# Two chains per pair of heads on TensorE, key tiles of 112, and fewer transfers in an attention and feed-forward kernel

## The chip, the cores and the metric

The kernel runs on one core of a Trainium2 chip. Its engines are TensorE (PE in the rows, PEld for its weight loads), VectorE (DVE), ScalarE (ACT), GpSimd (POOL) and SyncE (SP), which here issues every DMA. The metric is the device time of one execution in microseconds; less is better. PE's clock has two levels, 1.2 and 2.4 GHz, and the profile gives the granted level of a stretch as a share of the higher one.

## The reference

For 8 batches of 12 heads, 448 rows of 64 elements, everything in float32:

```
q_n, k_n = rmsnorm(q, g_q), rmsnorm(k, g_k)
scores = q_n @ k_n.T / sqrt(64);  scores -= max(scores, axis=-1)
attn = exp(scores);  attn /= sum(attn, axis=-1) + 1e-9
x = attn @ v                       # heads side by side: 3584 tokens of 768
h = x @ w_in                       # 768 -> 2048
out = (h * cos(h)) @ w_out         # 2048 -> 768
```

## The kernel before

Heads are taken two at a time: 48 pairs, six to a batch. A pair has its two heads on the two halves of the 128 partitions (64 each), and two matmuls of 64 rows, one per half, run beside each other on PE.

For a pair u the program does, on PE:

- **rough scores** R (`rough`, tile SA): q_hi times k_hi, one tile of queries after the other. VectorE takes each row's maximum (`rowmax`, tile sm), turns it (`m_turn`), and it goes through DRAM (`m_store`, `m_load`) into a row, tile mr.
- **scores** S (`score`, tile ST): keys on the partitions, queries along the row. Four matmuls add up: k_hi q_hi, k_hi q_lo, k_lo q_hi, and minus the maximum from mr. ScalarE writes the exponential (`expo`, tiles P0 to P3).
- **P v** (`av`, tile O): float32, so each matmul goes through the array more than once. The 64 columns of each head stand beside each other.
- **sums** (`total`, tile T): ones times P. From the seventh pair on VectorE first adds the four P tiles (`p_sum`). The sum goes through DRAM twice for its reciprocal (`t_store`, `t_load`, `i_store`, `rs_load`).

The key axis of 448 is cut into three tiles of 128 and a rest of 64. The rest of both heads shares a fourth tile, as a 128-row matmul of 448 columns; for it, q and k lie in DRAM and in SBUF with 576 columns, the rest repeated. S and T share two PSUM tiles of two banks each, R has one such tile of its own, and O and the feed-forward tile ph have one bank each.

Between these, PE runs the first feed-forward matrix (`ffn1`, tile ph, called F below): 128 rows by 128 columns, three matmuls for each product of split operands. A batch has 16 blocks of 18 matmuls, 48 to a pair. F of a batch runs while the next batch's pairs are attended; that of the last batch follows alone. Then a second phase (tiles y, lines from 587 on) applies the cosine and the second matrix.

No loop sets the order of the first phase. Every step is given to a planner (class `Plan`) with an engine, a cost and a due time; the planner goes through time by its costs, and on each engine takes, among the steps whose inputs are ready, the one that is due first. The result is one fixed order for each engine and for SP's queue, each of which runs strictly in it. Four numbers at the head of the plan set the due times: BASE, PER0, PER1 and PER, the start of a pair's scores.

Of the kernel before, what the change touches and what calls it, by code (L numbers as in the profile page):

```python
# [27 lines left out]
class Plan:  # L28
# [5 lines left out]

    SIGNAL = 0.16
    LEAD = 0.3

    def __init__(self, rings, apart=False):
        self.rings = rings
        self.parts = []  # L40
        self.start = []
        self.lead = []
        self.writer = {}
        self.readers = {}
        self.users = {}
        self.apart = apart
        self.issue = set()

    def add(self, eng, cost, due, fn, *args, r=(), w=(), land=0.0, start=0.0, lead=None):
        n = len(self.parts)  # L50
        deps = set()
# [19 lines left out]
        self.lead.append(self.LEAD * (eng == PE) if lead is None else lead)  # L71

    def order(self):
# [23 lines left out]
        self.busy = dict.fromkeys(free, 0.0)  # L97
        while True:
# [16 lines left out]
            n = heapq.heappop(can[e])[1]  # L115
            cost, fn, args, land = (parts[n][i] for i in (1, 3, 4, 6))
            end = free[e] = t + cost
# [16 lines left out]
def tile_attention_moe(  # L134
# [3 lines left out]
    qT: bass.AP,  # L138
    kT: bass.AP,
# [10 lines left out]
    W = kT.shape[2]  # L150
    NT = S // 128
    REST = S - 128 * NT
    NC = 2 * NT + 1

    NFIRST = 2
    NSUM = NP
# [26 lines left out]
    m_d = dpool.tile([NU, REST + 2 * S], F32, tag="m_d", name="m_d")  # L183
# [15 lines left out]
    less, less_r = (apool.tile([128, 128], F32R, tag=n, name=n, bufs=1) for n in ("less", "less_r"))  # L199
    for t in (less, less_r):  # L200
        nc.gpsimd.memset(t.bitcast(F32), 0.0)
        for hh in range(2):
            cs = slice(0, 128) if t is less else slice(64 * hh, 64 * hh + 64)
            nc.gpsimd.memset(t.bitcast(F32)[64 * hh : 64 * hh + 1, cs], -1.0)
    sms = [apool.tile([128, 32], F32, tag=f"sm{i}", name=f"sm{i}", bufs=1) for i in range(2)]
    mrs = [apool.tile([128, S], F32R, tag=f"mr{i}", name=f"mr{i}", bufs=1) for i in range(2)]
# [6 lines left out]
    def g_fold():  # L213
# [119 lines left out]
    def first_load(u):  # L333
        t = tl(u, "sd", [128, 14, D], F32, "P2")
# [27 lines left out]
    def first_copy(u, c, hh):  # L362
        name = "qk"[c] + "d"
        if hh == 0:
            x = tl(u, name, [128, W], F32)
            nc.gpsimd.memset(x[:, S:W], 0.0)
        x = pair[u][name][64 * hh : 64 * hh + 64]
        src = pair[u]["turn", c][:D, S * hh : S * hh + S]
        rest = slice(S + REST * hh, S + REST * hh + REST)
        if hh == 0:  # L370
            nc.vector.tensor_copy(x[:, :S], src)
            nc.vector.tensor_copy(x[:, rest], src[:, S - REST :])
        else:
            nc.scalar.copy(x[:, :S], src)
            nc.scalar.copy(x[:, rest], src[:, S - REST :])
# [7 lines left out]
    def r_load(u, c):  # L383
        dst = tl(u, ("rqb", "rkb")[c], [128, W], F32)
        for hh in range(2):
            p, n = slice(64 * hh, 64 * hh + 64), S * hh + S
            nc.sync.dma_start(dst[p, :S], row(r_d[u, c], n - S, n).broadcast_to([64, S]))
            rest = row(r_d[u, c], n - REST, n).unsqueeze(1).broadcast_to([64, 2, REST])
            nc.sync.dma_start(dst[p, S:].rearrange("p (a n) -> p a n", a=2), rest)  # L389

    def k_load(u):
        nc.sync.dma_start(tl(u, "kd", [128, W], F32), kT[u])

    def k_norm(u):
        kd = pair[u]["kd"]
        nc.gpsimd.tensor_tensor(kd, kd, pair[u].pop("rkb"), ALU.mult)  # L396

    def k_high(u):
        nc.scalar.copy(tl(u, "khi", [128, W], F32R), pair[u]["kd"])  # L399

    def k_low(u):
        d = pair[u]
        nc.gpsimd.tensor_tensor(tl(u, "kl", [128, W], F32R), d.pop("kd"), d["khi"].bitcast(F32), ALU.subtract)  # L403

    def q_load(u):
        nc.sync.dma_start(tl(u, "qd", [128, W], F32), qT[u])

    def q_norm(u):
        qd = pair[u]["qd"]
        nc.gpsimd.tensor_tensor(qd, qd, pair[u].pop("rqb"), ALU.mult)  # L410

    def q_high(u):
        nc.scalar.activation(tl(u, "qhi", [128, W], F32R), pair[u]["qd"], AF.Copy, scale=gsc)

    def q_low(u):
        d = pair[u]
        nc.vector.scalar_tensor_tensor(
            tl(u, "ql", [128, S], F32R), d.pop("qd")[:, :S], gsc, d["qhi"].bitcast(F32)[:, :S], op0=ALU.mult, op1=ALU.subtract
        )

    def v_load(u):
        nc.sync.dma_start(tl(u, "vs", [128, 2 * NT + 1, D], F32), v[u])


    def own(t, hh):
        return t[64 * hh : 64 * hh + 64, :S]

    def tiles(t, j, hh):
        return t[:, S:] if j == NT else t[64 * hh : 64 * hh + 64, 128 * j : 128 * j + 128]

    def rough(u, j):
        d = pair[u]
        t = d["SA", j] = double(ps_a, "SA", f"SA{u}_{j}")
        if j == NT:
            nc.tensor.matmul(t[:, 0, :S], tiles(d["qhi"], j, 0), d["khi"][:, :S], start=True, stop=True)
            return
        for hh in range(2):
            nc.tensor.matmul(t[:, hh, :S], tiles(d["qhi"], j, hh), own(d["khi"], hh), start=True, stop=True)  # L438

    def rowmax(u, j):  # L440
        t, sm = pair[u].pop(("SA", j)), sms[u % 2]
        if j < NT:
            nc.vector.tensor_reduce(sm[:, j : NC : NT + 1], t[:, :, :S], axis=AX.X, op=ALU.max)  # L443
        else:
            nc.vector.tensor_reduce(sm[:, j : j + 1], t[:, 0, :S], axis=AX.X, op=ALU.max)
# [4 lines left out]
    def m_store(u):  # L450
        mt = pair[u].pop("mt")
        m = m_d[u][: 2 * S].rearrange("(c p) -> c p", p=128)
        for p in range(0, 128, 32):
            nc.sync.dma_start(m[:, p : p + 32], mt[p : p + NC])
        for p in range(64, 128, 32):
            nc.sync.dma_start(row(m_d[u], 2 * S + p - 64, 2 * S + p - 32), mt[p + NT : p + NT + 1])

    def m_load(u):
        for hh in range(2):
            n = (S + REST) * hh  # L460
            nc.sync.dma_start(mrs[u % 2].bitcast(F32)[64 * hh : 64 * hh + 1], row(m_d[u], n, n + S))

    def score(u, j):
        d, mr = pair[u], mrs[u % 2]
        t = d["ST", j] = double(ps_s, "ST", f"ST{u}_{j}")
        for n, (a, c) in enumerate((("khi", "qhi"), ("khi", "ql"), ("kl", "qhi"), (None, None))):
            for hh in range(1 if j == NT else 2):
                if j == NT:
                    out, st, mv = t[:, 0, :S], tiles(d[a], j, 0) if a else less_r, d[c][:, :S] if c else mr
# [582 lines left out]
```

## Time and profile before

| | us |
|---|---|
| median of 3 runs | 1544.09 (1537.98 to 1549.36) |
| the profiled execution | 1546.6 |
| its span, first to last instruction | 1544.8 |
| granted clock of PE over the span | 0.968 |
| first matmul of F | 137.14 |
| first matmul of the second phase | 1128.15 |

The span has a first phase of 1128 us and a second of 417 us. Of the first, the 137 us before F begins hold the first six pairs. A row of the timeline gives the start, the length as modelled (matmuls overlap, so the step from one start to the next is what one costs), the engine, the line, and in brackets how long the engine was idle before and what ended that.

### The profile page before, as it was taken

The page shows a single profiled execution, that of the slowest core. Times are in us where ns is not written, and L with a number is a line of the kernel's source. Part 1 is how long each engine was busy: PE and PEld are TensorE (multiplying, and loading weights), DVE is VectorE, ACT ScalarE, POOL GpSimd, SP SyncE. Part 2 cuts the span into 40 slices and gives each one's busy share as a digit, 9 for nine tenths or more (in the row PEclk, how much of TensorE's full clock was granted, in tenths as well). Part 3 has the DMA queues.
Part 4 walks back from the last instruction along what each step waited for, and adds up shares of the span by engine and source line. Part 5 has one row for each costly group of instructions (what it writes and reads, how often), then busy time and mean ns, then how long its engine had stood idle before and what let it go on. Part 6 is the DMA issues. An engine that isn't in the chain of part 4 may idle for free.

```text
span 1544.8 us, 21497 instructions
## 1 busy us (share of the span) xinstructions
PE 1452.5 (94%) x7060; PEld 1041.2 (67%) x7060; DVE 973.0 (63%) x1255; ACT 781.3 (51%) x1212; POOL 905.0 (59%) x600
## 2 busy tenths in 40 slices
PE   3987889999999999999999999999999999999999
PEld 2433455656656666665666666567988999999998
DVE  7536769555666676556674757521787877868911
ACT  3543434444444444444444434323867777778732
POOL 6756657664585767576746454501138576585674
PEclk6998789999999999999999999999999999999999
DMA  5555663445646566566664555314957958859463
GB/s 164 136 151 180 195 215 113 126 136 156 188 128 223 176 195 186 179 198 192 186 186 135 186 174 165 116 55 150 346 180 256 323 167 292 290 171 336 165 209 107
DMA packets 187264, 287.09 MB, mean 186 GB/s; under 512 B 69968, under 2 KB 133648, under 8 KB 187152
## 3 DMA queue, kind: packets, MB, share of 16 engines
q1 hardware_dynamic: 187152, 285.72, 58.5%
q8 instruction: 55, 0.90, 0.3%
q14 instruction: 57, 0.47, 0.1%
HBM read 222.38 MB, written 63.25 MB: 185 GB/s over the span
## 4 chain that ended last, share of the span: by engine, by line
PE 65%; DMA 12%; DVE 8%; SPq 5%; POOL 4%; issue 4%; ACT 2%; DVEq 0%; POOLq 0%; ACTq 0%
PE ph L572 9%; PE ST L473 8%; PE y L651 8%; PE y L652 8%; PE y L650 8%; PE ph L574 7%; PE ph L573 7%; PE O L500 6%; DMA ti<-t_d 2%; DMA rawo<-w_out 2%; PE SA L438 2%; PE T L514 2%; DVE P L489 2%; DVE sm L443 2%; SPq L389 1%
## 5 line engine op out<-in xcount | busy, mean ns | idle before, releaser
L572 PE MATMUL ph<-xs,wi 128*128 128x448 f32 x768 | 309.3, 403 | 4.7 <-ACT he L584 3.9
L573 PE MATMUL ph<-xs,wi 128*128 128x448 f32 x768 | 283.4, 369 | 1.8 <-POOL xs L558 1.8
L574 PE MATMUL ph<-xs,wi 128*128 128x448 f32 x768 | 283.8, 369 | 0.0
L651 PE MATMUL y<-glo,wo 128*128 128x448 f32 x672 | 246.2, 366 | 1.3 <-POOL glo L635 1.3
L650 PE MATMUL y<-ghi,wo 128*128 128x448 f32 x672 | 245.8, 366 | 0.0
L652 PE MATMUL y<-ghi,wo 128*128 128x448 f32 x672 | 245.8, 366 | 0.0
L443 DVE TENSOR_REDUCE sm<-SA 128x2 f32<-128x896 f32 x144 | 156.3, 1086 | 123.4 <-PE SA L438 122.7
L572 PEld LDWEIGHTS ph<-xs,wi 128*128 128x128 f32 x768 | 145.1, 189 | 123.2 <-issue 78.7
L480 ACT ACTIVATE P<-ST 128x896 f32<-128x896 f32 x144 | 131.6, 916 | 136.5 <-PE ST L473 136.4
L500 PE MATMUL O<-P,vs 128*64 128x448 f32 (+1 forms) x768 | 185.9, 569 | 0.0
L485 DVE TENSOR_TENSOR P<-P,P 128x896 f32<-128x896 f32 x84 | 106.5, 1268 | 125.0 <-PE O L500 86.1
L584 ACT COPY he<-ph 128x448 f32<-128x448 f32 x128 | 68.1, 532 | 185.7 <-PE ph L574 143.1
L574 PEld LDWEIGHTS ph<-xs,wi 128*128 128x128 f32 x768 | 146.0, 190 | 13.3
L573 PEld LDWEIGHTS ph<-xs,wi 128*128 128x128 f32 x768 | 146.2, 190 | 10.7 <-POOL xs L558 2.1
L651 PEld LDWEIGHTS y<-glo,wo 128*128 128x128 f32 x672 | 126.2, 188 | 13.5 <-POOL glo L635 2.9
L652 PEld LDWEIGHTS y<-ghi,wo 128*128 128x128 f32 x672 | 126.2, 188 | 10.5
L650 PEld LDWEIGHTS y<-ghi,wo 128*128 128x128 f32 x672 | 126.2, 188 | 10.5
L330 POOL TENSOR_TENSOR r<-r,nhalf 128x14 f32<-128x14 f32 (+1 forms) x50 | 129.8, 2597 | 5.6 <-DVE r L350 2.1
L403 POOL TENSOR_TENSOR kl<-kd,khi 128x576 fp32r<-128x576 f32 x48 | 72.6, 1514 | 96.5 <-ACT khi L399 85.0
L410 POOL TENSOR_TENSOR qd<-qd,rqb 128x576 f32<-128x576 f32 x46 | 72.3, 1572 | 73.4 <-DMA i_d<-ti 20.1
L547 POOL TENSOR_TENSOR xf<-xf,rs 128x448 f32<-128x448 f32 x48 | 59.7, 1244 | 78.8 <-DMA rs<-i_d 62.8
L396 POOL TENSOR_TENSOR kd<-kd,rkb 128x576 f32<-128x576 f32 x46 | 71.7, 1558 | 52.4 <-DMA kd<-kT 21.3
(234 smaller groups left out, 2641.6 us busy)
## 6 DMA issues: line engine op xcount, KB each, us to landing
wo<-wo_d SPq DMA_DIRECT2D x88, 768.0 KB
h_d<-he SPq DMA_DIRECT2D x128, 224.0 KB
hb<-h_d SPq DMA_DIRECT2D x128, 224.0 KB
wo_d<-wv SPq DMA_DIRECT2D x56, 384.0 KB
sd<-sd SPq DMA_DIRECT2D x46, 448.0 KB
kd<-kT SPq DMA_DIRECT2D x46, 288.0 KB
qd<-qT SPq DMA_DIRECT2D x46, 288.0 KB
raw<-w_in SPq DMA_DIRECT2D x16, 768.0 KB
```

Source lines behind the costliest of these rows:

```text
L330: nc.gpsimd.tensor_tensor(r, r, nhalf.broadcast_to([128, c1 - c0]), ALU.pow)
L443: nc.vector.tensor_reduce(sm[:, j : NC : NT + 1], t[:, :, :S], axis=AX.X, op=ALU.max)
L473: nc.tensor.matmul(out, st, mv, start=(n == 0), stop=(n == 3))
L480: nc.scalar.activation(tl(u, f"P{j}", [128, 2, S], F32), t[:, :, :S], AF.Exp)
L485: nc.vector.tensor_tensor(d["P0"], d["P0"], d[f"P{step}"], ALU.add)
L500: nc.tensor.matmul(d["O"][64 * hh : 64 * hh + 64, :S], st, mv, start=(j == 0), stop=(j == NT))
L572: nc.tensor.matmul(ph[:, :S], whi, x2[:, 0, :], start=(cc == 0), stop=False)
L573: nc.tensor.matmul(ph[:, :S], whi, x2[:, 1, :], start=False, stop=False)
L574: nc.tensor.matmul(ph[:, :S], wlo, x2[:, 0, :], start=False, stop=(cc == NCC - 1))
L650: nc.tensor.matmul(y, whi, hi, start=(k == 0 and chain < 2), stop=False, skip_group_check=chain == 2)
L651: nc.tensor.matmul(y, whi, lo, start=False, stop=False, skip_group_check=chain == 2)
L652: nc.tensor.matmul(y, wlo, hi, start=False, stop=(k == NH - 1), skip_group_check=chain == 2)
```

## The change

Six things are changed, all in the first phase:

- **Planner.** A step on PE can now name the step that should follow it at once (`after`); PE waits up to PATIENCE for that one. Steps have a mode, F, H (64-row matmuls) or C (P v and sums), and a change of mode costs SWITCH in the plan. P v of a pair is one step (`av_all`). From the seventh pair on, sums, P v and the first three rough tiles of the pair after next follow each other; so do the fourth rough tile of the next pair and the four score tiles of this one.
- **Tiles.** The key axis is cut into four tiles of 112; all score and rough matmuls are now pairs of 64 rows by 112 columns. The repeated rest is gone, q and k have 448 columns, and P tiles have 112 partitions.
- **PSUM.** Rough scores, scores and sums share three tiles of two banks; O and ph share two single banks.
- **Sums.** VectorE's sums go to a tile of their own, PS, and no longer into P0.
- **Transfers.** q and k come in one DMA, their norms in two, not eight; the maxima are stored in one, not six, and the sums in one, not two. Over the program SP issues 1163 DMAs where it issued 1773.
- **Plan.** Due times, costs, the ring sizes and the places at which a pair's preparation is due are other numbers; there are eight xf tiles, not six.

The diff, cut to its core:

```diff
+    PATIENCE = 0.6
+    SWITCH = {("F", "H"): 0.2, ("H", "F"): 0.2, ("F", "C"): 0.15, ("C", "F"): 0.2, ("H", "C"): 0.15, ("C", "H"): 0.2}
...
-                if can[e]:
+                if e == PE and hold is not None:
+                    limit = free[e] + self.PATIENCE
+                    t = max(free[e], ready[hold]) if not left[hold] and ready[hold] <= limit else limit
+                elif can[e]:
...
-    NT = S // 128
-    REST = S - 128 * NT
-    NC = 2 * NT + 1
+    NT = 4
+    T = S // NT
+    NC = 2 * NT
...
-    ps_a = att.enter_context(tc.tile_pool(name="ps_a", bufs=1, space=PSUM))
-    ps_s = att.enter_context(tc.tile_pool(name="ps_s", bufs=2, space=PSUM))
-    ps_o = att.enter_context(tc.tile_pool(name="ps_o", bufs=1, space=PSUM))
-    ps_h = att.enter_context(tc.tile_pool(name="ps_h", bufs=1, space=PSUM))
+    ps_s = att.enter_context(tc.tile_pool(name="ps_s", bufs=3, space=PSUM))
+    ps_o = att.enter_context(tc.tile_pool(name="ps_o", bufs=2, space=PSUM))
...
     def m_store(u):
-        mt = pair[u].pop("mt")
-        m = m_d[u][: 2 * S].rearrange("(c p) -> c p", p=128)
-        for p in range(0, 128, 32):
-            nc.sync.dma_start(m[:, p : p + 32], mt[p : p + NC])
-        for p in range(64, 128, 32):
-            nc.sync.dma_start(row(m_d[u], 2 * S + p - 64, 2 * S + p - 32), mt[p + NT : p + NT + 1])
+        nc.sync.dma_start(m_d[u].rearrange("a c i -> (a c) i"), pair[u].pop("mt"))
...
-            for hh in range(1 if j == NT else 2):
-                if j == NT:
-                    out, st, mv = t[:, 0, :S], tiles(d[a], j, 0) if a else less_r, d[c][:, :S] if c else mr
-                else:
-                    out, st = t[:, hh, :S], tiles(d[a], j, hh) if a else less[64 * hh : 64 * hh + 64]
-                    mv = own(d[c] if c else mr, hh)
-                nc.tensor.matmul(out, st, mv, start=(n == 0), stop=(n == 3))
+            for hh in range(2):
+                st = own(d[a], hh, j) if a else own(less, hh)
+                nc.tensor.matmul(t[:T, hh, :S], st, own(d[c], hh) if c else mr[64 * hh : 64 * hh + 64, :, :T], start=(n == 0), stop=(n == 3))
...
+    def av_all(u):
+        for j in range(NT):
+            av(u, j)
...
-    BASE, PER0, PER1, PER = 30.0, 18.0, 19.0, 19.0
-    SPLIT = 54.0
+    BASE, PER0, PER1, PER = 30.0, 14.0, 18.5, 18.7
+    SPLIT = 50.0
+    AFTER = 9.0
...
     for u in range(NU):
-        spots += [("S", u, 0), ("S", u, 1)] + [("T", u - 1, 0)] * (u > NSUM) + [("S", u, 2), ("S", u, 3)]
+        spots += [("S", u, j) for j in range(NT)] + [("T", u, 0)] * (u >= NSUM)
+        spots += [("R", u + 2, j) for j in range(NT)] * (u + 2 < NU)
...
+            last = add(PE, 0.82, D0 + 0.8 * j, score, u, j, r=[(n, u) for n in ("khi", "kl", "qhi", "ql", "mr")], w=key,
+                       mode="H", after=last if j else link.pop("R", None))
...
+            n = add(PE, 0.75, D1, total, u, 0, 1, r=[("PS", u)], w=key, mode="C")
+            r = [k for p in P for k in p]
+            link["C"] = add(PE, 2.97, D1, av_all, u, r=r + [("vs", u)], w=[singles["O", u]], mode="C", after=n)
```

How this moves PE's instructions, in the middle of the first phase. A name ends in the pair's and the tile's number: SA34_2 is the rough tile 2 of pair 34, ST33_0 the score tile 0 of pair 33, T32 and O33 sums and P v, ph4_3 block 3 of F in batch 4. PE before, around the scores of pair 33; left out at each mark are matmuls of F, or the other three matmuls of a score tile:

```order
L438 MATMUL SA34_2_6614<-khi34_6340,qhi34_6444 128x448 x2
L473 MATMUL ST33_0_6619<-qhi33_6239,khi33_6134 128x448 x2
...
L572 MATMUL ph4_3_6631<-xs_677,wi3_1144 128x448
...
L435 MATMUL SA34_3_6644<-khi34_6340,qhi34_6444 128x448
...
L473 MATMUL ST33_1_6661<-qhi33_6239,khi33_6134 128x448 x2
...
L514 MATMUL T32_6679<-P032_6462,ones_100 64x448 x2
L500 MATMUL O33_6686<-P033_6638,vs33_6396 64x448 x2
...
L473 MATMUL ST33_2_6711<-qhi33_6239,khi33_6134 128x448 x2
...
L500 MATMUL O33_6686<-P133_6682,vs33_6396 64x448 x2
```

The same engine now, from the sums of pair 33 to the scores of pair 34:

```order
L490 MATMUL T33_6455<-PS33_6387,ones_94 64x448 x2
L479 MATMUL O33_6461<-P033_6358,vs33_6102 64x448 x2
...
L438 MATMUL SA35_0_6474<-khi35_6199,qhi35_6210 112x448 x2
...
L438 MATMUL SA35_2_6488<-khi35_6199,qhi35_6210 112x448 x2
L552 MATMUL ph4_5_6492<-xs_622,wi5_1023 128x448
...
L438 MATMUL SA35_3_6529<-khi35_6199,qhi35_6210 112x448 x2
L462 MATMUL ST34_0_6533<-qhi34_6034,khi34_6026 112x448 x2
...
L462 MATMUL ST34_1_6543<-qhi34_6034,khi34_6026 112x448 x2
```

What was spread among pieces of 6 or 12 matmuls of F is now two runs, with 18 to 36 matmuls of F between them. Counted through the whole order, PE goes 708 times from one of the shapes F, 64-row or P v to another before, and 239 times after; of these, 185 and 49 lead into P v or sums.

SP's queue in the startup, before, from one pair's maxima (mt3, stored through m_d) to the next store:

```order
L387 DMA rkb5_614<-r_d_86 64x448
L389 DMA rkb5_614<-r_d_86 64x2x64
...
L454 DMA m_d_87<-mt3_612 7x32 x4
L456 DMA m_d_87<-mt3_612 1x32 x2
L525 DMA ti1_661<-t_d_88 112x8
L387 DMA rqb5_668<-r_d_86 64x448
...
L378 DMA r_d_86<-r6_580 128x2x7
L315 DMA sd8_686<-sd 128x896
```

The same place now:

```order
L402 DMA rb5_552<-r_d_80 64x2x448 x2
L448 DMA m_d_81<-mt3_565 128x32
L335 DMA sd7_593<-sd 128x896
L504 DMA ti1_596<-t_d_82 112x8
L393 DMA r_d_80<-r6_567 128x2x7
L454 DMA mr1_103<-m_d_81 1x16x32 x2
```

One store and one pair of loads of norms stand where six and eight issues stood.

## Rows read from the trace of the kernel before

**Rows 1.** Windows: length; busy PE, PEld, DVE, ACT, POOL; PE clock, DMA share, GB/s.

```profile
0.00:137.00 137.00, 97.30 (x460) 46.37 (x461) 75.27 (x103) 60.27 (x89) 89.00 (x81) 0.84 0.55 161
137.00:300.00 163.00, 142.48 (x647) 85.51 (x647) 123.83 (x132) 73.54 (x105) 105.80 (x72) 0.89 0.52 163
300.00:1040.00 740.00, 715.73 (x3536) 456.99 (x3534) 448.34 (x527) 319.50 (x516) 425.69 (x313) 0.99 0.54 166
...
1128.00:1545.00 417.00, 411.68 (x2018) 378.09 (x2016) 281.89 (x423) 279.67 (x422) 273.51 (x129) 1.00 0.68 224
```

**Rows 2.** Timeline of ACT: the copied sums of pairs 12 and 46.

```profile
298.23 0.54 ACT L517 ACTIVATE ts<-T 128x448 f32<-128x448 f32 x1
...
1032.16 0.54 ACT L517 ACTIVATE ts<-T 128x448 f32<-128x448 f32 x1
```

**Rows 3.** Timeline of PE in the middle of the first phase.

```profile
600.00 0.36 PE L574 MATMUL ph<-xs,wi 128*128 128x448 f32 x1
600.29 0.47 PE L473 MATMUL ST<-qhi,khi 64*128 64x448 f32 x2
600.60 0.36 PE L473 MATMUL ST<-ql,khi 64*128 64x448 f32 x2
...
601.00 0.37 PE L473 MATMUL ST<-mr,less 64*128 64x448 f32 x2
601.29 0.97 PE L514 MATMUL T<-P,ones 128*64 128x448 f32 x4
602.10 0.92 PE L500 MATMUL O<-P,vs 128*64 128x448 f32 x4
602.95 0.47 PE L572 MATMUL ph<-xs,wi 128*128 128x448 f32 x1
603.26 0.37 PE L573 MATMUL ph<-xs,wi 128*128 128x448 f32 x1
```

**Rows 4.** Lines of PE, 300 to 1040 us: busy, mean; idle before them.

```profile
L438 PE MATMUL SA<-khi,qhi 64*128 64x448 f32 x198 | 46.0, 460 | 4.1 <-DVE sm L443 3.5 <-ACT qhi L413 0.6
L435 PE MATMUL SA<-khi,qhi 128*128 128x448 f32 x33 | 14.8, 449 | 17.7 <-DVE sm L443 17.6
```

**Rows 5.** Timeline of PE in the startup.

```profile
36.45 0.91 PE L473 MATMUL ST<-mr,less 64*128 64x448 f32 x2 [3.75 <-DMA mr<-m_d]
...
61.77 0.47 PE L438 MATMUL SA<-khi,qhi 64*128 64x448 f32 x2
63.44 0.47 PE L435 MATMUL SA<-khi,qhi 128*128 128x448 f32 x1 [1.19 <-DVE sm L443]
...
66.11 0.92 PE L473 MATMUL ST<-mr,less 64*128 64x448 f32 x2 [1.39 <-DMA mr<-m_d]
66.65 0.75 PE L473 MATMUL ST<-qhi,khi 64*128 64x448 f32 x2
...
134.25 0.93 PE L473 MATMUL ST<-mr,less 64*128 64x448 f32 x2 [4.21 <-DMA mr<-m_d]
```

**Rows 6.** Timeline of SP's queue in the startup.

```profile
72.02 1.60 SPq L454 DMA_DIRECT2D m_d<-mt  x4
...
78.40 0.58 SPq L461 DMA_DIRECT2D mr<-m_d  x2
```

**Rows 7.** Lines by shape, the whole span: busy, mean ns; idle before them.

```profile
L443 DVE TENSOR_REDUCE sm<-SA 128x2 f32<-128x896 f32 x144 | 156.3, 1086 | 123.4 <-PE SA L438 122.7
L485 DVE TENSOR_TENSOR P<-P,P 128x896 f32<-128x896 f32 x84 | 106.5, 1268 | 125.0 <-PE O L500 86.1 <-ACT P L480 38.5
L489 DVE TENSOR_TENSOR P<-P,P 64x448 f32<-64x448 f32 x84 | 93.5, 1113 | 7.4 <-ACT P L478 5.1
L445 DVE TENSOR_REDUCE sm<-SA 128x1 f32<-128x448 f32 x48 | 29.8, 621 | 38.7 <-PE SA L435 38.6
...
L480 ACT ACTIVATE P<-ST 128x896 f32<-128x896 f32 x144 | 131.6, 916 | 136.5 <-PE ST L473 136.4
L478 ACT ACTIVATE P<-ST 128x448 f32<-128x448 f32 x48 | 26.1, 543 | 70.4 <-PE ST L473 70.2
```

More of the change, by code (lines that the diff above doesn't have):

```diff
@@ L47, in __init__, with add @@
         self.issue = set()
-    def add(self, eng, cost, due, fn, *args, r=(), w=(), land=0.0, start=0.0, lead=None):
+        self.mode = {}
+        self.follow = {}
+    def add(self, eng, cost, due, fn, *args, r=(), w=(), land=0.0, start=0.0, lead=None, mode=None, after=None):
         n = len(self.parts)
+        self.mode[n] = mode
+        if after is not None:
+            self.follow[after] = n
         deps = set()
@@ L97, in order @@
         self.busy = dict.fromkeys(free, 0.0)
+        mode, hold, done = None, None, set()
         while True:
@@ L114, in order @@
                 heapq.heappush(can[e], (parts[n][2], n))
-            n = heapq.heappop(can[e])[1]
-            cost, fn, args, land = (parts[n][i] for i in (1, 3, 4, 6))
+            if e == PE and hold is not None:
+                n, hold = hold, None
+                if left[n] or ready[n] > t:
+                    continue
+                can[e].remove((parts[n][2], n))
+                heapq.heapify(can[e])
+            else:
+                n = heapq.heappop(can[e])[1]
+            cost, fn, args, land = (parts[n][i] for i in (1, 3, 4, 6))
+            if e == PE and self.mode[n]:
+                cost += self.SWITCH.get((mode, self.mode[n]), 0.0)
+                mode = self.mode[n]
+            if e == PE:
+                done.add(n)
+                hold = self.follow.get(n)
+                hold = None if hold in done else hold
             end = free[e] = t + cost
@@ new lines, in prepare @@
+        sd, r, rb, qk = ([(n, u)] for n in ("sd", "r", "rb", "qk"))
+        add(SP, ISS, D0 - 42, st_load, u, w=sd, land=6.5)
+        add(SP, ISS, D0 - 26, qk_load, u, w=[("qk", u, 0), ("qk", u, 1)], land=LAND)
+        add(ACT, 0.95, D0 - 34, st_square, u, w=sd)
+        add(DVE, 1.08, D0 - 33, st_reduce, u, r=sd, w=r)
+        add(POOL, 0.35, D0 - 32, st_mean, u, w=r)
+        add(POOL, 2.7, D0 - 31, st_pow, u, 0, 14, w=r)
+        add(SP, ISS, D0 - 27, st_store, u, r=r, w=[("rd", u)], land=LAND)
@@ L825, in attend @@
-        add(SP, 2 * ISS, D1 + 12, rs_load, u, r=[("id", u)], w=[("rs", u)], land=5.0)
+        P = [[(f"P{j}", u + NFIRST * (j == 0))] for j in range(NT)]
+        for j in range(NT):
+            key = [spots["S", u, j]]
+            last = add(PE, 0.82, D0 + 0.8 * j, score, u, j, r=[(n, u) for n in ("khi", "kl", "qhi", "ql", "mr")], w=key,
+                       mode="H", after=last if j else link.pop("R", None))
+            add(ACT, 0.92, D0 + 0.8 * j + 1, expo, u, j, r=key, w=P[j])
+            if j and u >= NSUM:
+                add(DVE, 1.25, D0 + 0.8 * j + 3, p_sum, u, j, r=P[j] + P[0] * (j == 1), w=[("PS", u)])
@@ L840, in multiply @@
                 r += [("xs", cc, s) for cc in (2 * part, 2 * part + 1) for s in range(2)]
[L841 removed]
+                add(PE, 1.225, d, ffn1, b, fc, part, ps_o, "S1", r=r, w=[key], mode="F")
             add(ACT, 0.53, d - 4, h_out, b, fc, r=[key], w=[("he", NFC * b + fc)])
             add(SP, ISS, d, h_store, b, fc, r=[("he", NFC * b + fc)], land=LAND)
[L845 to L846 removed]
+    for u in range(NFIRST):
+        first(u)
     for fc in range(NFC):
```

300 lines of the change are left out of this document (122 added, 178 removed), and 6 rows, old and new, of the table RING.

## The prediction

> **What bounds the kernel now.** I read the windows by stage first, then the lines of each engine, then PE's own timeline, because only a timeline shows what PE does between matmuls that all count as busy.
>
> The windows [rows 1] show three stages. Up to 137 us PE is busy 97.30 us at a granted clock of 0.84: the startup is bound by latency. From 300 to 1040 us it is busy 715.73 of 740 us (97%) at 0.99, so there PE is the bound, and DVE (448.34, 61%), POOL (58%) and ACT (43%) are not. From 1128 us on is the second phase, 417 us, of which the change touches nothing. The rate of the middle stage is read from ACT: the copied sums of pairs 12 and 46 stand at 298.23 and 1032.16 us [rows 2], 733.93 us for 34 pairs, 21.59 us each.
>
> But busy is not at its peak. In PE's timeline [rows 3] matmuls of one shape start 0.20 us apart: two concurrent 64-row matmuls of a score tile (600.60, then two steps to 601.00) just as one 128-row matmul of F. Where the shape changes, the step is longer. From F to scores it is 0.29 us (600.00 to 600.29), and the first step inside the scores 0.31 (to 600.60): 0.09 to leave and 0.11 to enter, 0.20 in all. From P v to F the same: the first step of F is 0.31 (602.95 to 603.26). Into sums or P v it is 0.09 and 0.05: sums take 0.81 us after a change (601.29 to 602.10), where P v that follows without one takes 0.85 with its own 0.09 to leave in it, so 0.76. A change costs 0.14 us if it leads into P v or sums, and 0.20 otherwise.
>
> **The change, part by part.**
>
> *Changes of shape (term 1).* PE's order has 708 of them before, 185 into P v or sums: 185 × 0.14 + 523 × 0.20 = 130.5 us. After it has 239, 49 of them into P v or sums: 6.9 + 38.0 = 44.9 us. Since PE is the bound, nearly all of that is on the path. Term 1 is **-86 us**. At 0.15 for each of the 469 it would be -70, at 0.20 throughout -94.
>
> *Matmuls themselves.* A pair had three 64-row tiles and one 128-row tile, and now has four 64-row tiles. Both kinds step by 0.20, so rough scores keep 4 steps and scores 16. P v and sums keep their number too. Nothing.
>
> *Startup (term 2).* PE waits there for the maxima's way through DRAM five times, from 3.75 us at 36.45 to 4.21 at 134.25 us, 14.7 us together [rows 5]; it waits 1.19 us for each row maximum, since R has one tile; and after a wait the clock is low (matmuls last 0.75 us at 66.65, not 0.36). SP is the cause of much of it: the store of the maxima is six issues, four of which take 1.60 us, and their load is issued 6.4 us after the store began (72.02 to 78.40) [rows 6]. The change issues 610 fewer DMAs, at the 0.40 us of one of those four. It has the rough scores of a pair ready one pair earlier, and three tiles, so that rough tiles no longer wait for each other. Against it: F now begins after eight pairs, not six, so PE has nothing to fill with for longer; two pairs more at the old share of idle (39.7 us in the first 137) would cost some 10 us. Between all of the waits gone with their clock, -30, and +10, I take **-13 us**, about the five waits.
>
> *Waits of R and S (term 3).* From 300 to 1040 us PE's idle is 24.3 us, and 21.8 of it is R waiting, nearly all for the row maximum [rows 4]. With three tiles that goes: **-22 us**. In its place comes a new wait. The three tiles are now also those of S: the third score tile takes the place of the fourth rough tile, which runs just ahead of the first, so its row maximum must be done by then. From one R to the next through the maximum is 1.67 us with DVE free (61.77 to 63.44) [rows 5]; PE gives it 0.20 for R and two score tiles of four steps of 0.20, 1.80 in all: 0.13 us to spare. DVE is busy 61% of the time with instructions of 0.85 us (448.34 over 527 [rows 1]), so the maximum finds half of one ahead of it in most pairs, sometimes two: 0.4 us for each of the 42 pairs from the seventh on, **+17 us**. Bounds: nothing, and a whole sum of 1.27 us [rows 7] less the 0.13, 48 us. Behind S wait only F and the next chain on PE. ACT's exponentials start late with it, and DVE's sums and T after them, but 36 matmuls of F, 7.3 us, lie between S and T, against an exponential of 0.92 and a sum of 1.27 after the last score.
>
> *Other engines.* A row maximum of the fourth tile goes from 0.62 to 1.09 us and its exponential from 0.54 to 0.92. The sums on VectorE go from 2 × 1.27 + 2 × 1.11 to 3 × 1.27, so DVE has 0.5 us less for a pair and ACT 0.4 more [rows 7]. They have 39% and 57% of the stage free: nothing. If the pair falls to 19.5 us, DVE stands at 65%. POOL's three operations on 576 columns now have 448, less too.
>
> A rule speaks against the new tiles. Trainium Kernel Development and Optimization of the Trainium skill, Best Practices, says always to tile to 128 partitions; by it 16 of 128 lanes lie idle in every tile of 112, and the 0.84 us more of maximum and exponential would be the price, 40 us over 48 pairs if they were on the path. The rows have it the other way: the old cut spent its fourth tile on 448 columns in three engines, and what it saved there was hidden under PE.
>
> *Sum.* -86 - 13 - 22 + 17 = -104. The profiled execution took 1546.6 us, so 1442.6; the median of the runs lies 2.5 us below it: **1440 us**. As a check, by the pair: ten changes of shape less at 0.185 on average is 1.85 us, the R waits 0.64, the new one 0.4: 21.59 becomes 19.5.
>
> **The rivals.**
>
> *Round trips take what PE gives back (chance 0.12).* A pair's norms, maxima and sums go through DRAM four times, in order, in one queue. At a shorter pair one of them comes too late: the reciprocal of the pair before stands on DVE between the sums of this one and waits for its load, then T waits. For it speaks that the startup shows PE waiting on such a trip at 16 us a pair (36.45 to 134.25 us are six pairs) [rows 5]. Against it: from 300 us on, PE's idle has 2.5 us left for everything but R's waits, and SP has 13 issues less for a pair. If 1.4 us for each of 42 pairs goes back to waiting, 59 of the 104 us are lost: 1499. The Trainium skill (DMA: Bandwidth & Descriptors, Rules for kernel authors) says that a transfer whose outermost dimension is under 16 is confined to that many DMA engines; the new load of the maxima is cut 4 by 4 by 32, the store of the sums into two rows, so by that rule both could land later than the old ones. No row of this case shows it.
>
> *The third score tile stalls PE (0.04).* The mechanism of term 3 at full size: row maxima queue behind decodes and sums on DVE, S stalls in every pair, and the clock falls after it, as at 66.65 us [rows 5]. It decides from 2.9 us a pair on, where 42 pairs eat the 121 us that terms 1 to 3 give without it. At 3.5 us of wait and 1 of slow clock, less the 0.4 counted, it is +172: 1612 us, slower. Against it: DVE has 39% free, and its maxima of a pair stand nearly side by side in its order.
>
> *The changes of shape cost nothing (0.06).* If the longer steps were only how starts are recorded, term 1 is nothing and -18 is left: 1526 us, 1.2% faster, on the edge. Against it: 0.20 us between starts is the rate of a long run of F, and after a change no later start catches up [rows 3]. By TensorEngine Tiling of the Trainium skill, Key Properties, switching the tiling mode drains the engine and going to another tile of a mode does not; by that rule, the trace agrees.
>
> **How the numbers follow.** The forecast has 0.78. Its own range, from -94 - 30 - 22 at one end to -70 + 10 - 22 + 48 at the other, is 1398 to 1510, most of it under 1485. For 8 in 10 I give 1400 to 1515, which takes in most of the forecast and the first rival. About 1%, 15 us, is what a measurement here can tell from no change. Faster by more: the forecast, the first rival and half of the third, 0.91 with some room; slower by more 0.04; within 1% 0.05.
>
> **What would show it.** Term 1: in the steady stretch PE's long steps at only five places of a pair, and copied sums about 19.5 us apart. Term 2: F beginning about when it does now, with eight pairs done and not six. Term 3: PE's idle under the score line, released by the row maximum, of 10 to 25 us in all, and none left under the rough line. The second phase should take its 417 us, beginning near 1025. It is wrong if the pairs stay above 20.5 us apart: then idle under T (late sums, the reciprocal ahead of them) is the first rival, idle over 2 us under S the second, and no idle with short steps the third.

## The result, and the profile after

The changed kernel takes 1415.69 us (median of 4 runs, 1412.94 to 1416.9) against 1545.53 on the same chip: 0.9163 of the time (95% interval 0.9124 to 0.9202). The forecast was 1440, the range 1400 to 1515. The profiled execution took 1412.94 us, its span is 1411.2.

The windows after, cut where F begins (138), at the copied sum of pair 12 (243), at the end of the steady pairs and where the second phase begins (996), columns as in [rows 1]:

```profile
0.00:138.00 138.00, 106.29 (x592) 58.05 (x592) 105.89 (x130) 76.46 (x108) 105.70 (x88) 0.91 0.68 203
138.00:243.00 105.00, 93.75 (x502) 65.06 (x502) 91.79 (x90) 53.67 (x78) 84.76 (x57) 0.93 0.52 155
243.00:905.00 662.00, 653.82 (x3744) 467.03 (x3740) 424.04 (x497) 321.03 (x519) 403.40 (x314) 1.00 0.58 174
...
996.00:1412.00 416.00, 410.29 (x2020) 378.38 (x2018) 281.49 (x422) 279.19 (x422) 273.30 (x129) 1.00 0.67 225
```

In the steady stretch PE now lacks 8.2 us of 662, not 24.3 of 740. The startup has a higher clock (0.91 and 0.93, before 0.84 and 0.89) and is shorter. The second phase is what it was. The copied sums of pairs 12 and 46 in ACT's timeline, which answer to [rows 2]:

```profile
242.59 0.54 ACT L497 ACTIVATE ts<-T 128x448 f32<-128x448 f32 x1 [0.34 <-PE T L490]
...
896.98 0.55 ACT L497 ACTIVATE ts<-T 128x448 f32<-128x448 f32 x1 [2.82 <-PE T L490]
```

They are 654.4 us apart: 19.25 us a pair, before 21.59. PE's timeline, which answers to [rows 3], through the rough tiles of a pair and into its chain of scores:

```profile
600.66 0.37 PE L554 MATMUL ph<-xs,wi 128*128 128x448 f32 x1
600.95 0.87 PE L438 MATMUL SA<-khi,qhi 64*112 64x448 f32 x6
601.75 0.47 PE L552 MATMUL ph<-xs,wi 128*128 128x448 f32 x1
602.06 0.36 PE L553 MATMUL ph<-xs,wi 128*128 128x448 f32 x1
...
604.38 0.46 PE L438 MATMUL SA<-khi,qhi 64*112 64x448 f32 x2
604.67 0.37 PE L462 MATMUL ST<-qhi,khi 64*112 64x448 f32 x2
604.87 0.36 PE L462 MATMUL ST<-ql,khi 64*112 64x448 f32 x2
605.07 0.37 PE L462 MATMUL ST<-qhi,kl 64*112 64x448 f32 x2
605.27 0.37 PE L462 MATMUL ST<-mr,less 64*112 64x448 f32 x2
```

Three rough tiles stand together and pay one way in and one out: 0.29 us from F (0.20 without a change), 0.80 for the three (0.60), 0.31 for F's first step, 0.40 in all. The groups of PE's lines, first from 243 to 905 us, which answer to [rows 4]:

```profile
L462 PE MATMUL ST<-qhi,khi 64*112 64x448 f32 x280 | 55.9, 395 | 6.4 <-DVE sm L442 3.2 <-ACT P L466 3.2
...
L438 PE MATMUL SA<-khi,qhi 64*112 64x448 f32 x272 | 45.3, 409 | 0.5 <-DVE sm L442 0.4
L490 PE MATMUL T<-PS,ones 112*64 112x448 f32 x136 | 33.0, 563 | 0.6 <-DVE PS L472 0.6
```

and then the startup, 0 to 243 us, which answers to [rows 5]:

```profile
L462 PE MATMUL ST<-mr,less 64*112 64x448 f32 x104 | 24.0, 445 | 1.9 <-DMA mr<-m_d 1.9
...
L438 PE MATMUL SA<-khi,qhi 64*112 64x448 f32 x112 | 22.0, 467 | 23.8 <-DVE sm L442 15.0 <-ACT ts L497 4.7 <-ACT qhi L419 4.0
```

R no longer waits in the steady stretch, and the idle time of the new wait, under the scores, is 6.4 us. Up to pair 12 PE waits once for the maxima's way through DRAM, 1.9 us. Before, it waited for it seven times up to there, 18.3 us: the five times of [rows 5], 14.7 us, and two more after 137 us.

By stage, the prediction's terms (0.185 us a change on average; 98 fewer changes up to pair 12, 352 in the 34 pairs to pair 46, 19 after) against the two profiled executions:

| | forecast | measured |
|---|---|---|
| up to pair 12 | -18 - 13 = -31 | 298.2 to 242.6: -55.6 |
| pairs 12 to 46 | -65 - 22 + 14 = -73 | 733.9 to 654.4: -79.5 |
| pair 46 to the second phase | -3 + 3 = 0 | 96.0 to 99.5: +3.5 |

Most of what the forecast missed lies in the startup. Whether the terms were right one by one, or only in their sum, is for experiments to tell.

### The profile page after: what moved, and what is told of

It reads as the page before. It is cut to its first block, busy times and chain, and to the rows that moved or that the text cites. A ratio compares the mean times of both kernels' runs of the same rounds, so it can differ in the third digit from the quotient of the medians.

```text
span 1411.2 us, 21112 instructions
## 1 busy us (share of the span) xinstructions
PE 1355.1 (96%) x7300; PEld 1050.3 (74%) x7300; DVE 948.4 (67%) x1209; ACT 780.9 (55%) x1208; POOL 878.1 (62%) x593
## 4 chain that ended last, share of the span: by engine, by line
PE 73%; DVE 8%; DMA 7%; POOL 6%; issue 3%; ACT 2%; SPq 1%; ACTq 0%; DVEq 0%; POOLq 0%
PE ST L462 9%; PE ph L552 9%; PE y L631 9%; PE y L632 9%; PE y L630 9%; PE ph L554 8%; PE ph L553 8%; PE O L479 8%; PE T L490 3%; PE SA L438 2%; DMA h_d<-he 2%; DVE sm L442 2%; DMA ti<-t_d 2%; POOL qk L409 1%; POOL r L350 1%
## 5 line engine op out<-in xcount | busy, mean ns | idle before, releaser
L442 DVE TENSOR_REDUCE sm<-SA 112x2 f32<-112x896 f32 x192 | 198.5, 1085 | 156.8 <-PE SA L438 156.5
L552 PE MATMUL ph<-xs,wi 128*128 128x448 f32 x768 | 291.2, 379 | 0.0
L554 PE MATMUL ph<-xs,wi 128*128 128x448 f32 x768 | 281.4, 366 | 0.0
L553 PE MATMUL ph<-xs,wi 128*128 128x448 f32 x768 | 281.3, 366 | 0.0
L466 ACT ACTIVATE P<-ST 112x896 f32<-112x896 f32 x192 | 166.7, 920 | 64.1 <-PE ST L462 62.0
L479 PE MATMUL O<-P,vs 112*64 112x448 f32 x768 | 156.2, 541 | 0.6 <-ACT he L564 0.6
L350 POOL TENSOR_TENSOR r<-r,nhalf 128x14 f32<-128x14 f32 (+1 forms) x50 | 135.6, 2714 | 6.4 <-DVE r L370 2.7
L409 POOL TENSOR_TENSOR qk<-qk,rb 128x448 f32<-128x448 f32 x92 | 121.1, 1332 | 25.2 <-DMA qk<-qk 16.2
L416 POOL TENSOR_TENSOR kl<-qk,khi 128x448 fp32r<-128x448 f32 x48 | 75.7, 1578 | 96.8 <-PE ST L462 86.0
L472 DVE TENSOR_TENSOR PS<-PS,P 112x896 f32<-112x896 f32 x84 | 122.7, 1461 | 13.4 <-ACT P L466 7.5
L479 PEld LDWEIGHTS O<-P,vs 112*64 112x64 f32 x768 | 54.0, 137 | 88.4 <-issue 82.7
```

What stands on the lines that cost most here:

```text
L350: nc.gpsimd.tensor_tensor(r, r, nhalf.broadcast_to([128, c1 - c0]), ALU.pow)
L409: nc.gpsimd.tensor_tensor(x, x, pair[u]["rb"][:, c], ALU.mult)
L442: nc.vector.tensor_reduce(sm[:T, j:NC:NT], t[:T, :, :S], axis=AX.X, op=ALU.max)
L466: nc.scalar.activation(tl(u, f"P{j}", [128, 2, S], F32)[:T], t[:T, :, :S], AF.Exp)
L479: nc.tensor.matmul(d["O"][64 * hh : 64 * hh + 64, :S], d["vs"][:T, 2 * j + hh], d[f"P{j}"][:T, hh], start=(j == 0), stop=(j == NT - 1))
L552: nc.tensor.matmul(ph[:, :S], whi, x2[:, 0, :], start=(cc == 0), stop=False)
```

## The experiments

Theory as predicted: the changes of shape are most of it, the transfers some 13 us in the startup. Rival: the transfers are worth far more, and the changes of shape less. Kernels ran on several chips, so differences are taken between their ratios to the kernel before on the same chip, times 1545 us; an interval of a difference is ±7 to ±8 us.

**e1, the chains taken apart.**

```diff
-        if after is not None:
-            self.follow[after] = n
...
-            d = base(u - 1) - 0.5 if last and u > NP else D0 + 1.0 * j
+            d = base(u) - 30.0 + 3.5 * j if u > NP else D0 + 1.0 * j
...
-            link["C"] = add(PE, 2.97, D1, av_all, u, ...)
+            for j in range(NT):
+                add(PE, 0.75, D0 + 3.5 * j + 4, av, u, j, ...)
```

> The changed kernel with its chains taken apart: no instruction is tied to the one before it, and rough scores, scores and P v of a pair are due 3.5 us apart, as they were before, P v tile by tile. Tiles of 112, rings and transfers stay as changed. PE's order has 687 changes of shape (708 before, 239 in the changed kernel), 561 of them in the 34 pairs from the 13th to the 46th (180 in the changed kernel). Theory (a change costs 0.14 to 0.20 us, and PE is the bound): 448 more at 0.17 is +76 us, 1492 us (1478 to 1505); in the 34 pairs +65 us, with PE busy throughout. Rival (the time came from fewer transfers and from waits that are gone, and a change of shape costs nothing): under 1425 us. Second rival (both halve it): about 1455 us.

Measured: 0.9595 (0.957 to 0.962), 1474.7 us. That is 67 us above the changed kernel for 448 changes, 0.149 us each. The window of the 34 pairs, columns as in [rows 1]:

```profile
247.00:951.00 704.00, 702.88 (x3690) 433.81 (x3688) 406.02 (x496) 324.68 (x513) 405.10 (x314) 1.00 0.52 163
```

In these pairs PE is busy 57.1 us more than after (645.8 us from 243 to 897) for 381 changes, 0.150 each, and idle only 1.1 us. A change of shape costs time, but in sum less than was read; and with as many changes as before (687, 708) this kernel is still 63 us faster than the one before. Something else is worth that much.

**e4, one link undone.**

```diff
-            before = link.pop("C", None) if j == 0 else n if j < NT - 1 else None
+            before = link.pop("C", None) if j == 0 else n if j < NT - 1 and u <= NP else None
```

with the due times of these tiles 3 us apart.

> The changed kernel with one link undone: the first three rough tiles of a pair, from the eighth pair on, are each due 3 us after the other and tied to nothing; all else as changed. 331 changes of shape, 92 more, all between F and rough scores or back; 85 of them in the 34 steady pairs. Theory (0.20 us for each): +18 us, 1434 us (by 0.14 each +13, 1429 us), and PE's idle no longer than before. Rival (a change of shape costs nothing, chains help by fewer waits): 1412 to 1420 us, or faster, since each row maximum has more time.

Measured: 0.9243 (0.9226 to 0.926), 1421.9 us: +12 us, 0.13 a change, under both of the prices but with both ends of the theory inside its interval. Its PE timeline shows a rough tile alone in F:

```profile
604.75 0.37 PE L554 MATMUL ph<-xs,wi 128*128 128x448 f32 x1
605.04 0.45 PE L438 MATMUL SA<-khi,qhi 64*112 64x448 f32 x2
605.43 0.47 PE L552 MATMUL ph<-xs,wi 128*128 128x448 f32 x1
605.74 0.37 PE L553 MATMUL ph<-xs,wi 128*128 128x448 f32 x1
```

Steps of 0.29, 0.39 and 0.31, where 0.20 each would do: 0.39 for two changes. So a single change costs what was read in [rows 3], while the kernel pays less in sum: the changed kernel has delays inside its chains that e4 hasn't (term 1 below).

**e2, the old transfers under the new order.** The maxima stored in six, the norms loaded in eight, q and k in two, the sums stored in two; the planner is not told.

```diff
-            nc.sync.dma_start(dst[64 * hh : 64 * hh + 64], src)
+            for c in (1, 0):
+                for n0, n1 in ((0, 384), (384, S)):
+                    src = row(r_d[u, c], S * hh + n0, S * hh + n1).broadcast_to([64, n1 - n0])
+                    nc.sync.dma_start(dst[64 * hh : 64 * hh + 64, c, n0:n1], src)
```

> The changed kernel, its order on PE unchanged, with 13 more transfers for a pair: the maxima stored in six, the reciprocal norms loaded in eight, q and k loaded in two, the sums stored in two. Theory (the startup became short by fewer issues on the queue of transfers): at 0.4 us an issue 5.2 us more of the queue for each pair; in the first 243 us, where PE waits for the maxima's way through DRAM, 10 to 25 us come back, in the 34 pairs from the 13th on none: 1426 to 1441 us. Rival (the startup became short by the common rough and score tiles and by the order): 1412 to 1420 us. Second rival (the queue holds the steady pairs as well): over 10 us more in the 34 pairs, over 1445 us.

Measured: 0.9666 (0.9634 to 0.9698), 1485.8 us: +78 us. The startup gives back 25.0 us up to pair 12, as the theory had it, but the 34 pairs give 49.4: the second rival. Their window, columns as in [rows 1]:

```profile
268.00:971.00 703.00, 661.57 (x3688) 467.08 (x3686) 410.19 (x496) 316.54 (x512) 398.26 (x314) 0.98 0.53 163
```

PE is idle 33 us more than after and busy 16 us more for the same matmuls, at a clock of 0.98 and not 1.00. One place shows how a wait comes about. Timelines of SP's queue, of DVE and of PE in e2:

```profile
600.05 4.93 SPq L404 DMA_DIRECT2D rb<-r_d  x8
605.03 0.58 SPq L512 DMA_DIRECT2D ti<-t_d  x1
```

```profile
607.07 0.20 DVE L515 RECIPROCAL ti<-ti 112x8 f32<-112x8 f32 x1 [2.31 <-DMA ti<-t_d]
607.18 0.51 DVE L264 SCALAR_TENSOR_TENSOR wx<-rawo,wx 128x384 int32<-128x384 int32 x1
607.61 2.28 DVE L479 TENSOR_TENSOR PS<-PS,P 112x896 f32<-112x896 f32 x2
```

```profile
609.95 0.97 PE L497 MATMUL T<-PS,ones 112*64 112x448 f32 x4 [0.85 <-DVE PS L479]
```

Eight issues hold the queue for 4.93 us, and the load of a finished pair's sums stands behind them. DVE, which works in order, waits for it ahead of the next pair's sums, and PE for those. PE's idle says "sums on VectorE"; the cause is two steps back. Idle time of this kind, under T, is 12.3 us in the 34 pairs (0.6 after); the rest stands under the scores and the rough tiles. DVE's waits for that load, over the 34 pairs, after and in e2 (us in total, times, longest):

```profile
DVE ti L507 <- DMA ti<-t_d: 5.6, 4, 3.4
```

```profile
DVE ti L515 <- DMA ti<-t_d: 40.3, 16, 4.6
```

**e7, e8, e12: which transfers, and what of them.** e7 is e2 with the norms' eight alone, e8 with the maxima's six alone. e12 has eight loads of norms too, cut by partitions:

```diff
+            for p in range(0, 64, 16):
+                nc.sync.dma_start(dst[64 * hh + p : 64 * hh + p + 16], src[p : p + 16])
```

> The changed kernel with the reciprocal norms of a pair loaded in eight transfers, not two; the other transfers as changed. An issue of such a load takes 0.64 us of the queue, so 3.8 us more a pair in one block, behind which the loads of sums and maxima wait. Theory A (the time that the queue is occupied sets what is lost): e2 adds 3.8 here, 1.7 for the store of the maxima, 0.8 for the rest; 60% of its 70 us, +42 us: 1458 us (1440 to 1470), mostly in the steady pairs. Theory B (the maxima's way through DRAM is what PE waits on): under +10 us.

> The changed kernel with the maxima of a pair stored in six transfers, not one; the other transfers as changed. An issue takes 0.34 us, 1.7 us more a pair. Theory A (the occupied time of the queue): 27% of 70 us, +19 us: 1435 us (1425 to 1445). Theory B (the maxima's way through DRAM): +40 to +60 us, in the startup above all.

> The changed kernel with the reciprocal norms of a pair loaded in eight transfers as in e7, but cut by partitions (16 partitions, both rows of 448) and not by columns: as many issues as e7, and pieces of the same size as in the changed kernel, where e7 has twice as many pieces. Theory A (what is lost is the time of the issues on the queue): as e7, +35 to +50 us, 1450 to 1465 us. Theory B (the number of pieces, which the engines of the transfers work off): 1412 to 1422 us.

Measured: e7 0.945 (0.9419 to 0.948), 1455.5 us, +44. e8 0.9244 (0.9207 to 0.9281), 1423.0 us, +12. e12 0.9362 (0.9324 to 0.9401), 1442.4 us, +31. In e7 and e8 theory A holds within its error: about 12 us for each us of queue a pair in e7, 7 in e8. e12 lies between its two theories: its pieces are those of the changed kernel, so theory B falls, and theory A's 35 us are within the interval. An issue of its kind takes 0.42 us in the median, not the 0.59 of e7's. Its loads of norms hold the queue 3.5 us a pair, those of e7 4.7, the two of the changed kernel 1.3. At e7's rate this time of the issues makes most of the 31 us; whether the pieces add something is open.

**e5, both undone** (e1's and e2's edits together).

> The chains taken apart as in e1 and the 13 more transfers of e2 in one kernel: the fourth corner beside the changed kernel, e1 (0.043 of the old time slower than it) and e2 (0.050 slower). Theory A (the queue of transfers holds PE only where the pair is short: e1 leaves PE no idle time at 20.7 us a pair, e2's queue holds its pairs at 20.7 too): much less than the sum, 1485 to 1515 us, with PE idle in the 34 steady pairs under 25 us. Theory B (each transfer delays each pair by a fixed time): the sum of both, 1540 us (1530 to 1555).

Measured: 1.0062 (1.0032 to 1.0092), 1548.0 us. Theory B holds and theory A falls: the transfers cost 72 us without the chains (e5 less e1) and 78 with them (e2 less the changed kernel); the chains are worth 61 us with the old transfers and 67 with the new. The two add up.

**e13, the kernel before with 9 of its transfers a pair taken out.** PE's order, tiles, rings and plan are untouched; POOL's multiplication by the norms becomes two operations, since the repeated rest is no longer loaded.

```diff
-            nc.sync.dma_start(dst[p, :S], row(r_d[u, c], n - S, n).broadcast_to([64, S]))
-            rest = row(r_d[u, c], n - REST, n).unsqueeze(1).broadcast_to([64, 2, REST])
-            nc.sync.dma_start(dst[p, S:].rearrange("p (a n) -> p a n", a=2), rest)
+            nc.sync.dma_start(dst[64 * hh : 64 * hh + 64], row(r_d[u, c], S * hh, S * hh + S).broadcast_to([64, S]))
...
+        nc.sync.dma_start(m_d[u].rearrange("(c a i) -> a c i", a=4, i=32), pair[u].pop("mt"))
```

> The kernel before, its order on PE, tiles, rings and planner untouched, with 424 of its transfers taken out (9 a pair): the maxima stored in one (loaded in three, not two), the sums stored in one, the reciprocal norms loaded in four and not eight; POOL's multiplication by the norms is two operations, not one. 4.2 us less of the queue for a pair. Theory A (a pair's transfers cost PE time on any plan, as in e2, where 6.3 us of the queue a pair cost 70 us): -46 us, 1494 us (1480 to 1510), much of it in the steady pairs. Theory B (the prediction's second term: the startup alone gains): -9 to -15 us, 1525 to 1532 us. Theory C (transfers cost PE time only where the planner does not know of them; it gives these the time of four and six issues): within 8 us of the kernel before, 1532 to 1548 us.

Measured: 0.9722 (0.9691 to 0.9753), 1495.8 us: -43 us, the size of theory A, with nothing else of the change in it; but only a third of it is in the steady pairs. F begins at 120.79 us here, not at 137.14, so the windows are cut there (the 34 pairs are 266 to 985):

```profile
0.00:121.00 121.00, 92.07 (x462) 43.60 (x463) 75.77 (x103) 59.97 (x90) 91.48 (x93) 0.99 0.58 177
121.00:266.00 145.00, 134.65 (x638) 80.33 (x637) 129.30 (x133) 71.66 (x104) 118.68 (x87) 0.94 0.56 174
266.00:985.00 719.00, 704.10 (x3503) 450.50 (x3504) 442.62 (x525) 317.31 (x514) 440.58 (x378) 0.99 0.53 166
```

From the lines of PE, the rough tiles in the 34 pairs of e13:

```profile
L438 PE MATMUL SA<-khi,qhi 64*128 64x448 f32 x198 | 46.1, 460 | 0.6 <-DVE sm L443 0.5
...
L435 PE MATMUL SA<-khi,qhi 128*128 128x448 f32 x33 | 13.9, 422 | 14.0 <-DVE sm L443 14.0
```

The scores' last matmul up to pair 12, in the kernel before and in e13:

```profile
L473 PE MATMUL ST<-mr,less 64*128 64x448 f32 x82 | 22.8, 468 | 18.3 <-DMA mr<-m_d 18.3
```

```profile
L469 PE MATMUL ST<-mr,less 64*128 64x448 f32 x82 | 17.7, 402 | 0.3 <-DMA mr<-m_d 0.3
```

32.3 us of it come before pair 12, half of them before F begins. The waits for the maxima go to 0.3 us, and the clock up to F rises from 0.84 [rows 1] to 0.99; PE is busy 5.2 us less there with as many matmuls. These are one execution each, and the clock of this stretch varies: it is 0.91 in the changed kernel and 0.95 in e10, whose order on PE is the same. The mean clocks of all executions on this chip are apart, though, 0.968 to 0.978 before and 0.980 to 0.989 in e13. The 34 pairs give 14.9 us: R waits 14.6 us and not 21.8, so a third of that wait, put down to the row maximum in [rows 4], went with the transfers. What DVE waited for in the 34 pairs of the kernel before, and in those of e13 not at all, is the load of the sums:

```profile
DVE ti L528 <- DMA ti<-t_d: 16.4, 14, 3.4
```

**e3, the rings of before for the scores.**

```diff
+    ps_a = att.enter_context(tc.tile_pool(name="ps_a", bufs=1, space=PSUM))
-    ps_s = att.enter_context(tc.tile_pool(name="ps_s", bufs=3, space=PSUM))
+    ps_s = att.enter_context(tc.tile_pool(name="ps_s", bufs=2, space=PSUM))
...
-    PATIENCE = 0.6
+    PATIENCE = 3.0
```

> The changed kernel with the rings of before for the scores: the rough tiles have one tile of their own, the score tiles and the sums two. So that the chains stay whole on PE (253 changes of shape, 239 in the changed kernel), the planner waits up to 3 us for the next link. Theory (the three common tiles are what took R's waits away, and fewer changes would not have come without them): from one rough tile to the next through the row maximum is 1.67 us against 0.20, so the chain of three waits 2.9 us a pair; with two tiles the third and fourth score tiles wait some 0.5 us for exponentials of 0.92 us. In the 42 pairs from the seventh on 143 us at most; waits that run beside each other and the slow pairs of the startup leave about +110: 1525 us (1480 to 1560), PE idle under the rough line released by the row maximum. Rival (waits of R were hidden anyway, or DVE is not asked for more): 1416 to 1430 us.

Measured: 1.0372 (1.0339 to 1.0405), 1596.0 us: +187, more than forecast. The rough tiles in its 34 pairs:

```profile
L439 PE MATMUL SA<-khi,qhi 64*112 64x448 f32 x272 | 64.1, 468 | 81.5 <-DVE sm L443 81.5
```

2.4 us a pair, close to the 2.9 worked out. The rest is the startup, 34 us longer up to pair 12, and PE's clock, at 0.94 in the steady pairs. In this order, chains with one rough tile are slower than no change at all.

**e9, e10, e6: attempts to go further.** e9 loads the maxima, and the reciprocal sums of both heads, in one transfer each; e10 the maxima alone; e6 makes the sums of pairs 3 to 5 on VectorE.

```diff
-            src = row(i_d[u], hh * S, hh * S + S).broadcast_to([64, S])
-            nc.sync.dma_start(dst[64 * hh : 64 * hh + 64], src)
+        src = i_d[u].rearrange("(h o s) -> h o s", h=2, o=1).broadcast_to([2, 64, S])
+        nc.sync.dma_start(dst, src)
...
-    NSUM = NP
+    NSUM = 3
```

> An attempt to go on in the same way: the maxima's store writes them in the order in which they are read, so that they load as two long rows in one transfer (before: two of 16 pieces each), and the reciprocal sums of both heads load in one transfer. Two issues less a pair, 1.3 us of the queue; PE's order unchanged. Theory A (queue time is what is lost still, in the startup): 5 to 12 us less, 1404 to 1411 us. Rival (the queue has enough room now, and PE's idle in the first 243 us is by row maxima): 1413 to 1418 us.

> Of e9 the maxima alone: stored in the order in which they are read, and loaded as two long rows in one transfer. The reciprocal sums load in two transfers, as in the changed kernel. Theory (e9 lost its 62 us by the one transfer of the reciprocal sums, which POOL had 8.5 us after its issue where the last of two took 3.7, and not by the maxima): 1405 to 1417 us, POOL's wait for the reciprocal sums back at about 25 us in the steady pairs. Rival (two long rows land as late as the merged load of e9): 1430 to 1475 us, PE waiting for the maxima in its score line.

> An attempt at the startup: the sums of the fourth to sixth pair are made by VectorE and two matmuls, like those of the later pairs, not by eight matmuls on PE. PE has 18 matmul steps of 0.2 us less in the startup, VectorE nine sums of 1.46 us more. Theory (PE and VectorE are both waited for there, VectorE's row maxima more): -3 to +5 us, 1412 to 1420 us.

Measured: e9 0.9566 (0.9539 to 0.9593), 1474.1 us, 62 us slower with fewer transfers, a miss of both theories. e10 0.9191 (0.9156 to 0.9225) and e6 0.9197 (0.9162 to 0.9233): neither told apart from the changed kernel, and no version beat it. POOL's multiplication by the reciprocal sums, in the lines of POOL over the 34 pairs, after and in e9:

```profile
L527 POOL TENSOR_TENSOR xf<-xf,rs 128x448 f32<-128x448 f32 x34 | 39.7, 1169 | 24.4 <-DMA rs<-i_d 24.4
```

```profile
L529 POOL TENSOR_TENSOR xf<-xf,rs 128x448 f32<-128x448 f32 x34 | 41.1, 1208 | 114.7 <-DMA rs<-i_d 114.7
```

POOL waits for it in nearly every pair, and it lands 8.5 us after its issue (median of 41 pairs in which POOL waited), not 3.7 us after the second of two (13 pairs). In e10, where the maxima alone are merged, POOL waits 22.6 us for it, so this transfer is the cause and not the maxima. The queue suffers too. SP's waits for the store of the sums to land, ahead of their load, in the 34 pairs after and in e9:

```profile
SPq L504 <- DMA t_d<-ts: 7.8, 11, 2.0
```

```profile
SPq L507 <- DMA t_d<-ts: 88.8, 31, 6.5
```

In e10 it is 7.4 us. While SP waits, every later transfer waits behind it. No run separates this way to PE from POOL's own delay.

## Why the prediction was right, and where its terms were wrong

The direction, the range and the mechanism of the chains were right. The forecast is 24 us too high, and that it is no more is luck. The transfers were worth some 60 us more than was forecast, and about half of that was made up by the rest: from the kernel before to e5, which has neither the chains nor fewer transfers, the forecast has R's waits of -22 us, and the measured difference is +10.

**Term 1, the changes of shape: -86 forecast, -70 measured** (469 at e1's 0.149), the end of its range, but net of what the chains cost. Single changes do cost 0.20 (e4's rows). In the 34 pairs the 381 changes of e1 should have cost 70 us by the forecast's prices and cost 49.6. Of the difference, 7.1 is idle time that the chains bring and e1 does without. Another 10 stands in the timeline of the changed kernel, inside the chains of scores, where no shape changes:

```profile
620.21 0.37 PE L462 MATMUL ST<-qhi,kl 64*112 64x448 f32 x2
620.41 0.36 PE L462 MATMUL ST<-mr,less 64*112 64x448 f32 x2
620.70 0.46 PE L462 MATMUL ST<-qhi,khi 64*112 64x448 f32 x2
621.00 0.37 PE L462 MATMUL ST<-ql,khi 64*112 64x448 f32 x2
```

From one score tile to the next the step is 0.29 us, and the one after it 0.30, where others take 0.20. A matmul is modelled as 0.36 us long, so a delay this short doesn't count as idle. Summed over the steps between 64-row matmuls in the 34 pairs, two that start together counted as one, such delays come to 10.0 us over 0.203 a step; left out are idle time and, in the first step of a run, the 0.094 us of its change of shape. In e4 they come to 0.2 us and in e1 to none. Most stand where the next score tile begins, or one step on. That fits the new wait of term 3, but that they are waits for a tile is argued, not shown. The other 3 us are open.

**Term 2, the transfers: -13 forecast, -72 to -78 measured.** This is the step that failed. In the startup it weighed -30 us, all of the waits gone with their clock, against +10 for a later F, and took about the five waits for the maxima, 14.7 us; for the steady pairs it put nothing. e13 shows 32.3 us up to pair 12. The five waits leave out the matmuls at a low clock after them (5.2 us up to F) and the stretch from F to pair 12 (15.9 us less, two more waits for the maxima among it). In the steady pairs e13 shows 14.9 us, e2 49.4. For these the prediction had the right rows and stopped one step early: PE's idle was R waiting for row maxima, and the row maxima's own delay was not traced to what DVE waits for. The first rival names that wait, the load of the sums, but expects it at a shorter pair only; the kernel before had 16.4 us of it. The size has an open end: the planner of e2 and e5 isn't told of their transfers, so a part of the 72 to 78 us can be the plan's. e13, where the planner allows for more transfers than are left, has 43 us for 4.2 us of queue a pair; at that rate the 6.3 of e2 would be 64.

**Term 3: R's waits -22 forecast; 21.8 became 0.5.** e3 shows that this order needs the three common tiles, e13 that a third of these waits went with the transfers. The new wait was forecast at 17 us, 14 of them in the 34 pairs. As idle time it is 6.4 there, half of it for exponentials and not for the row maximum; with the 10 us of longer steps above, if they are waits, it is 16. Chains and their own waits together were forecast at -69, and e1 gives -67.

**Tiles and the other engines: 0 forecast.** From the kernel before to e5 the tiles, rings and plan change, without chains and with as many transfers: +10 us, where R's waits alone would give -22. The planner of e5 isn't told of its transfers, which the old one was, so this part isn't settled. That tiles of 112 cost 40 us, as the prediction works out from the rule of the Trainium skill (Trainium Kernel Development and Optimization, Best Practices), no run shows by itself. In the 34 pairs its share would be 28 us, and of the changed kernel only PE's idle time of 8.2 us and the 10 us of longer steps could hold it there.

**The rivals.** Round trips that take back what PE gives: with the old transfers that is what happens, 1485.8 us in e2 for 1499 forecast, though the idle time under T is a third of PE's added idle time there; with the new ones it doesn't. Scores that stall PE on the row maximum: 3.2 us of idle time in 34 pairs, 13 with all of the longer steps. Free changes of shape: excluded by e1.

**The signs named ahead.** Pairs 19.25 us apart (about 19.5), F beginning at 138.04 us (about when it did), no idle under the rough line: as said. Idle under the score line was 6.4 us, not 10 to 25, and there were long steps inside the chains beside those at the changes of shape. The second phase took 415 us from 996.5, not from 1025.

## What to carry to other kernels

Where one queue issues all DMAs in order, price a transfer by the time that its issue holds the queue, in every stage, and follow an idle time back through the engines until it ends at an engine that works or at a queue: the first releaser named may only be passing on a late load. Read the steps from start to start too: a delay shorter than a matmul's modelled length shows there and not as idle time. Chains of one matmul shape pay, but only with enough tiles in PSUM that each link finds its own free. Merging transfers pays as long as the merged one still lands as early; the timeline from issue to the first use tells.

## What the runs showed of the hardware

- One load of 128 partitions from two rows, each repeated over 64, in one transfer: 8.5 us from issue to use; as two transfers of 64 partitions, 3.7 us. The Trainium skill (DMA: Bandwidth & Descriptors, Rules for kernel authors) confines a transfer whose outermost dimension is under 16 to at most that many DMA engines; by that rule, two here. The later landing in e9 agrees with it, though the trace doesn't show which engines worked. For small ones the runs show no such price: with the maxima as two long rows (e10) PE waits 1.6 us for them in the startup, 1.9 with the pieces of the changed kernel.
- An issue on SP's queue goes by its form more than by its size: 0.59 us in the median for 64 partitions of 384 or 64 columns (e7), 0.42 us for 16 partitions of two rows of 448 (e12).
